# Attention and a gated feed-forward on one core: the first block's second product in another order, a cast and a copy on other engines

## The chip, the core and the metric

The kernel runs on one core of one Trainium2 chip. The core has TensorE (matrix products and transposes, PE in the profile; its weight loads are shown as PEld), VectorE (DVE), ScalarE (ACT), GpSimd (POOL) and SyncE (SP), which work side by side and wait for each other by semaphores; sixteen DMA engines move data. Products are written to PSUM, everything else lies in SBUF. The metric is the device time of one execution in microseconds.

## The reference

A recurrent attention (a decaying state per head) feeds a feed-forward block:

```python
def _attn_ref(q, k, v):                       # (4, 8, 768, 64)
    gamma = 1.0 - 2.0 ** (-5.0 - np.arange(H))
    for t in range(S):
        state = gamma[None, :, None, None] * state + np.einsum('bhd,bhe->bhde', k[:, :, t], v[:, :, t])
        y[:, :, t] = scale * np.einsum('bhd,bhde->bhe', q[:, :, t], state)

def _moe_ref(x, w_in, w_out):                 # x (3072, 512), w_in (512, 2048), w_out (2048, 512)
    h = x @ w_in
    g = h * np.tanh(softplus(h))
    return g @ w_out
```

The input of the second part is the output of the first, with the heads side by side: 4 · 768 = 3072 tokens of 8 · 64 = 512 values.

## The kernel before

**Tiling.** The tokens are cut into 24 chunks of 128. Within a chunk the recurrence is done by products: scores (k against q), a mask, `present` (masked scores times v) and `past` (the state before the chunk times q); `outer` gives what the chunk adds to the state. Chunks go through the feed-forward in blocks: block 0 has four chunks (0 to 3), each of the ten blocks behind it two. `y_two(blk)` makes the attention output of the two chunks of a block, which ScalarE copies to `xt`, the input of the block's first product.

**The two products.** The first product (`g1` for block 0, `g1_seven` for the others) gives h, to which ScalarE applies the activation and writes `g`. The second is `first_g2` for block 0 and `seven` for the others. `g1_seven`, `seven` and `first_g2` save products by sums: of the eight products of quarter matrices some or all are replaced by seven on sums and differences (Strassen and Winograd), which VectorE forms in float16: `tmats` from `w_out` (L549 to L552, the four steps of `weight_sums`), `gsums` from `g`. In `first_g2` that is done for two pairs of chunks (`pairs`) and, of the four slices of 512 rows of `w_out`, for slices 0 and 2 in the main; slices 1 and 3 go in as plain products.

**Order.** The order on every engine is the order in which the program text issues the work (`manual_schedule`); each engine takes its instructions in that order, and waits are added where data or buffers need them. `late` is a list of VectorE steps (the sums of the weights), of which `some_late(n)` issues the next n. `steps` of `g1_seven` and `seven` is a table that says which side work is issued at which named place of a block; `steps_of_first` is that of block 1. `gate(x)` is a small GpSimd copy that holds GpSimd's queue until x is there.

**PSUM.** Two pools of buffers: `mmps`, four banks, and `atps`, two buffers of two banks. In `first_g2` each pair p has two banks: `t0[p]` holds pb and pe (halves of a bank), `t1[p]` holds px and pz. A product that writes one half of a bank waits for a copy that reads the other half. The scores, the transposes, u (outer products) and y take turns in the two `atps` buffers.

**Around the change in `first_g2`.** TensorE's groups are `mm(...)`, four products per pair. Behind px (L939) ScalarE copies it out (L940). pz (L944), then pe (L946), copied as `m5` (L947). `cast_wout(2, FPS // 2)` (L948) turns slice 2 of `w_out` to float16: VectorE the first half (L184), ScalarE the second (L186). L550, the second sum of the weights, needs that slice; a gate waits for L550, and behind it GpSimd casts q (L336) and v (L347) of chunk 4, asks for k of chunk 6 (L342), and goes on with chunk 5, k of chunk 7, chunk 6. `turn(g, on_act)` transposes q and k of a chunk on TensorE (L381, L383) and copies the result to `qkt`, by ScalarE (L386) or VectorE (L388). `scores_one` is `scores` (L397) and `mask` (L403). `outer_wide(4)` (L441) and L445, L449 make the state behind chunk 4. Near the end come four groups `end(p, i)` with slice 3 of `w_out`, which ScalarE casts whole (L186, two instructions), and `y_two(1)` (L463 present, L412 outer, L454 past, L499 the copy of `xt`) ahead of the last group. Block 1 then begins with L629.

**In block 1** `spread_next` (L435, two ScalarE copies) lays the state of chunk 6 out for `past`; `sums_a` (L572, L573), `sums_b` (L700) and `sums_c` (L704) form the sums of g.

Of the kernel before, what the change touches and what calls it, by code (L numbers as in the profile page):

```python
# [16 lines left out]
def kernel(  # L17
# [161 lines left out]
    def cast_wout(s, on_act=0):  # L179
        src = wtmps.pop(("out", s))  # L180
        t = wouts[s] = cpool.tile([P, FPS, d_model], FP16, name=f"wout{s}")
        n = FPS - on_act
        if n:
            nc.vector.tensor_copy(t[:, :n], src[:, :n])  # L184
        for f in range(n, FPS, 2):
            nc.scalar.copy(t[:, f:f + 2], src[:, f:f + 2])  # L186
# [152 lines left out]
    def bring_k(g):  # L339
        if g < NCK:  # L340
            b, c = divmod(g, NCH)
            nc.gpsimd.dma_start(  # L342
                room16(g)[1], k[b, :, c * C:(c + 1) * C].rearrange("h p d -> p h d"))
# [6 lines left out]
    def casts(g):  # L350
        cast_q(g)
        cast_v(g)
# [119 lines left out]
    def scores_one(g):  # L472
        scores(g)
        mask(g)
# [7 lines left out]
    def outer_two(blk):  # L482
        gs = handed_on(blk)
        if gs:
            u_ps = u_tile()
        for j, g in enumerate(gs):
            outer(g, u_ps[:, j, :, :D])

    def y_two(blk):
        a = first[blk]  # L490
        y_ps = atps.tile([P, HP, 2, C], FP32, name="y_ps", tag="at")
        for j in range(2):
            present(a + j, lambda i: y_ps[:, i, j], j == 0)
        outer_two(blk)
        for j in range(2):
            if (a + j) % NCH > 0:
                past(a + j, lambda i: y_ps[:, i, j])
        xts[blk] = xtp.tile([P, HP, TB], FP16, name="xt")
        nc.scalar.copy(  # L499
            xts[blk][:, :, :2 * C], y_ps.rearrange("p i j c -> p i (j c)"))  # L500
# [33 lines left out]
    def some_late(n):  # L534
        for _ in range(min(n, len(late))):
            late.pop(0)()
# [360 lines left out]
    def first_g2():  # L897
# [11 lines left out]
        def a(p, i, s):  # L909
            return lambda f: gts[0, s * FPS + f][:, (2 * p + i) * P:(2 * p + i + 1) * P]  # L910
# [4 lines left out]
        def b(s, j):  # L915
            return lambda f: wouts[s][:, f, j * hf:(j + 1) * hf]
# [4 lines left out]
        def mm(o_ps, x, w, first=False, last=False):  # L921
            for f in range(FPS):
                nc.tensor.matmul(  # L923
                    o_ps, x(f), w(f), start=first and f == 0, stop=last and f == FPS - 1,
                    skip_group_check=True)
# [15 lines left out]
        g_sum(1, g_part(0, 1), g_part(2, 1), ALU.add)  # L941
        g_sum(2, the_sum(1), g_part(0, 0), sub)
        for p in pairs:
            mm(pz[p], a(p, 1, 1), b(1, 1))  # L944
        for p in pairs:
            mm(pe[p], sm(p, 1), t(1), True)  # L946
            nc.scalar.copy(m5[p], pe[p])  # L947
        cast_wout(2, FPS // 2)  # L948
        some_late(1)
        gate(tmats[0][:, 1, 0, :1])  # L950
        casts(CPB)
        bring_k(CPB + 2)
        some_late(1)
        g_sum(3, g_part(0, 0), g_part(0, 1), sub)
        g_sum(4, g_part(2, 0), the_sum(2), sub)
        some_late(1)
        for p in pairs:
            mm(pb[p], a(p, 0, 1), b(1, 0))
        for p in pairs:
# [7 lines left out]
        for p in pairs:  # L967
            mm(px[p], sm(p, 3), t(3))
            nc.vector.tensor_tensor(osb[p][1][:, 1], px[p], m5[p], op=ALU.add)
        casts(CPB + 1)  # L970
        bring_k(CPB + 3)
        for p in pairs:
            mm(pe[p], sm(p, 4), b(2, 1))
        scores_one(CPB)
        some_late(1)
        turn(CPB + 1, True)
        cast_wout(3, FPS)
        for p in pairs:
            mm(px[p], a(p, 1, 2), t(4))
# [9 lines left out]
        def end(p, i):  # L989
            mm((t0, t1)[i][p], a(p, i, 3), lambda f: wouts[3][:, f], last=True)  # L990
            if i == 0:
                nc.vector.tensor_tensor(osb[p][0], t0[p], osb[p][0], op=ALU.add)
            else:
                nc.vector.tensor_tensor(osb[p][1][:, 1], pz[p], osb[p][1][:, 1], op=ALU.add)
                nc.scalar.copy(osb[p][1][:, 0], px[p])
            row0 = (2 * p + i) * P
            stores.append((1, out[row0:row0 + P], osb[p][i].rearrange("p j c -> p (j c)")))

        end(0, 0)
        end(0, 1)  # L1000
        end(1, 0)
        y_two(1)
        end(1, 1)

    def turn_and_load(g):
# [43 lines left out]
    def steps_of_first(blk):  # L1049
        a, nb = first[blk] + 4, blk + 1  # L1050
        return {
            "p2": [(gate_x, blk), (cast_v, a - 1), (bring_k, a), (sum_next, a - 2)],
            "p6": [(turn_and_load, a - 1), (some_late, 1)],
            "p7": [(cast_q, a), (some_late, 1), (spread_next, a - 2),
                   (sums_a, blk, slice(0, FPS))],
            "p4": [(cast_v, a), (bring_k, a + 1), (some_late, 1), (store, 2),
                   (sums_a, blk, slice(FPS, FPS + 2))],
            "end": [(turn_and_load, a), (store, 2), (sums_a, blk, slice(FPS + 2, 2 * FPS))],
            "m1": [(scores, a - 2), (scores, a - 1), (mask, a - 2)],
            "m2": [(gate_g, blk), (cast_q, a + 1), (cast_v, a + 1), (bring_k, a + 2),  # L1060
                   (mask, a - 1), (turn_and_load, a + 1)],
            "m7": [(y_two, nb)],
            "m3": [(x_sums, nb)],
        }
# [39 lines left out]
```

## Time and profile before

| | |
|---|---|
| Runs before | 202.73, 202.76, 203.03 us; median 202.76 |
| The profiled execution | 203.02 us, of which the span of the profile is 201.2 |
| Granted TensorE clock, mean | 1.00 |
| TensorE busy | 191.6 us, 95% of the span |
| `first_block` up to the first row of `first_g2` | 0 to 33.07 us |
| `first_g2` with `y_two(1)` | 33.07 to 52.01 us |
| Block 1 | 52.01 to 67.59 us |
| Blocks 2 to 10 | 67.59 us to the end |

How to read it: times are microseconds from the start of the span. A row of the view in order of time gives start, length, engine, line of the kernel, operation, what is written from what, the form and a count; several like instructions in a row are merged, the length then runs from the first start to the last end. In brackets stands how long the engine sat idle before, and whose result ended that. A TensorE row's length contains a modelled tail, so successive rows overlap; the distance between starts is what a product costs. A few records of products can be missing, which shows in the counts.

```profile
DVE  2777798597679669568478587597498597596462
ACT  2363666444692494594674685675664774765740
POOL 7072006396454435636706518608606705110000
...
DMA  5999999999999997997997997998995955301102
```

These are four lines of the page's part with the span in 40 equal slices (about 5 us each), busy share in tenths: `first_g2` is the seventh slice to the tenth. VectorE has 9 of 10 in one of them and 7 or 8 in others; the DMA engines are busy throughout up to half the span.

### The profile page before, as it was taken

How to read it: one execution, taken by the hardware profiler on the slowest of the kernel's cores; microseconds unless marked ns; L12 is line 12 of the kernel's file. 1: busy time of each engine (PE TensorE's matmuls, PEld its weight loads, DVE VectorE, ACT ScalarE, POOL GpSimd, SP SyncE). 2: the span in 40 equal slices, each digit the busy share in tenths (PEclk: the TensorE clock that was granted, in tenths of full speed). 3: DMA queues.
4: the chain of work that ended last, by engine and by line, in shares of the span. 5: the costliest groups of instructions: out<-in, count | busy, mean ns of one | idle time of the engine just before them, and what ended most of it. 6: DMA issues, size and time to landing. Idle time of an engine off the chain costs nothing.

```text
span 201.2 us, 5722 instructions
## 1 busy us (share of the span) xinstructions
PE 191.6 (95%) x2363; PEld 158.1 (79%) x2363; DVE 142.9 (71%) x293; ACT 116.8 (58%) x222; POOL 81.9 (41%) x110
## 2 busy tenths in 40 slices
PE   6897999989999999999999999999999999999993
PEld 2455545775788888988988988988988988988982
DVE  2777798597679669568478587597498597596462
ACT  2363666444692494594674685675664774765740
POOL 7072006396454435636706518608606705110000
PEclk9999999999999999999999999999999999999999
DMA  5999999999999997997997997998995955301102
GB/s 176 300 313 356 384 387 287 218 285 168 236 197 222 184 186 147 195 141 149 206 144 163 185 138 152 192 131 158 183 204 116 203 85 46 114 5 50 58 26 78
DMA packets 95897, 36.05 MB, mean 179 GB/s; under 512 B 82304, under 2 KB 89984, under 8 KB 95872
## 3 DMA queue, kind: packets, MB, share of 16 engines
q1 hardware_dynamic: 74928, 33.04, 70.8%
q0 software_dynamic: 20800, 2.62, 20.4%
q8 instruction: 18, 0.29, 0.6%
q14 instruction: 7, 0.06, 0.1%
q10 hardware_dynamic: 144, 0.03, 0.1%
HBM read 27.30 MB, written 6.29 MB: 167 GB/s over the span
## 4 chain that ended last, share of the span: by engine, by line
PE 82%; ACT 6%; DVE 4%; DMA 2%; POOL 2%; issue 2%; DVEq 0%; POOLq 0%
PE o_ps L726 30%; PE h_ps L653 17%; PE h_ps L629 15%; PE h_ps L514 6%; PE y_ps L463 3%; PE at L397 2%; PE y_ps L454 2%; DMA qfirst<-in_q_dram 2%; PE o_ps L923 2%; ACT wout L186 1%; POOL qk L336 1%; PE h_ps L797 1%; PE u_ps L412 1%; DVE gsum L704 1%; DVE qfirst L211 1%
## 5 line engine op out<-in xcount | busy, mean ns | idle before, releaser
L653 PE MATMUL h_ps<-xt,win 128*128 128x256 f16 x320 | 41.5, 273 | 0.0
L646 DVE TENSOR_TENSOR hsum<-h_ps,hsnap 128x512 f32<-128x512 f32 x30 | 19.8, 687 | 22.3 <-PE h_ps L629 19.9
L726 PEld LDWEIGHTS <-gsum 128*128 128x128 f16 x320 | 30.8, 98 | 4.1 <-DVE gsum L704 0.6
L653 PEld LDWEIGHTS <-win 128*128 128x128 f16 x320 | 29.3, 98 | 3.6
L726 PE MATMUL o_ps<-tmat,gsum 128*128 128x256 f16 x240 | 27.8, 273 | 0.0
L726 PEld LDWEIGHTS <-g 128*128 128x128 f16 x240 | 23.2, 98 | 3.3 <-ACT g L660 0.4
L640 ACT ACTIVATE g<-hsum 128x512 f16<-128x512 f32 x30 | 18.6, 630 | 11.6 <-DVE hsum L646 11.6
L403 DVE TENSOR_TENSOR am<-at,tri 128x1024 f16<-128x1024 f32 x20 | 24.3, 1215 | 0.1
L347 POOL TENSOR_TENSOR v<-vf,qvs 128x512 f16<-128x512 f32 x20 | 23.5, 1173 | 0.2 <-DMA vf<-in_v_dram 0.2
L660 ACT ACTIVATE g<-h_ps 128x512 f16<-128x512 f32 x40 | 22.9, 603 | 0.8 <-PE h_ps L653 0.6
L636 ACT COPY hsnap<-h_ps 128x512 f32<-128x512 f32 x30 | 16.4, 580 | 11.3 <-PE h_ps L629 11.3
L355 POOL COPY gate<-gsum 128x1 f16<-128x1 f16 x9 | 1.6, 181 | 49.7 <-DVE gsum L700 49.7
L336 POOL TENSOR_TENSOR qk<-qf,qvs 128x512 f16<-128x512 f32 x20 | 21.2, 1060 | 0.9 <-DMA qf<-in_q_dram 0.9
L740 DVE TENSOR_TENSOR osb<-o_ps,snap 128x256 f32<-128x256 f32 x30 | 12.5, 418 | 12.5 <-PE o_ps L726 11.0
L732 ACT COPY snap<-o_ps 128x256 f32<-128x256 f32 x30 | 11.2, 373 | 16.0 <-PE o_ps L726 15.7
L629 PEld LDWEIGHTS <-wsum 128*128 128x128 f16 x320 | 19.6, 98 | 0.5
L726 PE MATMUL o_ps<-wout,g 128*128 128x256 f16 x160 | 19.4, 273 | 0.1
L342 POOL DMA_DIRECT2D qk<-in_k_dram x20 | 18.8, 942 | 0.0
L499 ACT CAST xt<-y_ps 128x1024 f16<-128x1024 f32 x10 | 10.1, 1012 | 11.9 <-PE y_ps L454 11.9
L629 PE MATMUL h_ps<-xsum,wsum 128*128 128x128 f16 x240 | 16.7, 219 | 0.0
L629 PEld LDWEIGHTS <-win 128*128 128x128 f16 x240 | 15.1, 98 | 1.1 <-issue 0.5
L435 ACT COPY stx<-stc 64x256 f16<-64x256 f16 x30 | 12.0, 399 | 2.0 <-POOL stc L429 1.8
(118 smaller groups left out, 308.4 us busy)
## 6 DMA issues: line engine op xcount, KB each, us to landing
vf<-in_v_dram SPq DMA_DIRECT2D x24, 256.0 KB, 5.6
out_dram<-osb SPq DMA_DIRECT2D x22, 256.0 KB, 4.9
qf<-in_q_dram SPq DMA_DIRECT2D x20, 256.0 KB, 4.8
wt<-in_moe_w_out_dram SPq DMA_DIRECT2D x3, 1024.0 KB, 8.6
qk<-in_k_dram POOLq DMA_DIRECT2D x20, 128.0 KB, 5.3
wi<-in_moe_w_in_dram SPq DMA_DIRECT2D x4, 512.0 KB, 7.3
wi<-in_moe_w_in_dram SPq DMA_DIRECT2D x2, 1024.0 KB, 11.3
qfirst<-in_q_dram SPq DMA_DIRECT2D x2, 512.0 KB, 5.0
```

The source lines that it names most:

```text
L336: nc.gpsimd.tensor_tensor(room16(g)[0], loaded[g][0], qs.unsqueeze(2).broadcast_to((P, H, D)), op=ALU.mult)
L342: nc.gpsimd.dma_start(room16(g)[1], k[b, :, c * C:(c + 1) * C].rearrange("h p d -> p h d"))
L347: nc.gpsimd.tensor_tensor(room16(g)[2], loaded[g][2], vs.unsqueeze(2).broadcast_to((P, H, D)), op=ALU.mult)
L403: nc.vector.tensor_tensor(am, ats.pop(g), tri.unsqueeze(1).unsqueeze(1).broadcast_to((P, 2, HP, C)), op=ALU.mult)
L629: nc.tensor.matmul(h_ps[:, f], w(f, d), x(d), start=first and f == 0 and d == 0, stop=d == n - 1, skip_group_check=True)
L636: nc.scalar.copy(x, h_ps)
L640: nc.scalar.activation(gt[:, 2 * i * FPS:(2 * i + 1) * FPS, j * P:(j + 1) * P], h, AF.Mish, scale=inv_boost3)
L646: nc.vector.tensor_tensor(h, h_ps, x, op=ALU.add)
L653: nc.tensor.matmul(h_ps[:, j], win(s, 2 * half + j, bp), xt(blk, bp), start=bp == 0, stop=bp == NBP - 1)
L660: nc.scalar.activation(gt[:, fb:fb + 2], h_ps, AF.Mish, scale=inv_boost3)
L726: nc.tensor.matmul(o_ps, x(f), w(f), start=first and f == 0, stop=f == n - 1, skip_group_check=True)
L740: nc.vector.tensor_tensor(dst, o_ps, plus, op=ALU.add)
```

## The change

It touches `first_g2`, the place of the outer products of `y_two(1)`, and the table of block 1.

```diff
-    def y_two(blk):
+    def y_two(blk, hand_on=True):
...
-        outer_two(blk)
+        if hand_on:
+            outer_two(blk)
...
         for p in pairs:
-            mm(pz[p], a(p, 1, 1), b(1, 1))
-        for p in pairs:
             mm(pe[p], sm(p, 1), t(1), True)
             nc.scalar.copy(m5[p], pe[p])
-        cast_wout(2, FPS // 2)
+        cast_wout(2)
         some_late(1)
         gate(tmats[0][:, 1, 0, :1])
         casts(CPB)
-        bring_k(CPB + 2)
+        cast_q(CPB + 1)
         some_late(1)
         g_sum(3, g_part(0, 0), g_part(0, 1), sub)
         g_sum(4, g_part(2, 0), the_sum(2), sub)
         some_late(1)
+        for p in pairs:
+            mm(pz[p], a(p, 1, 1), b(1, 1))
         for p in pairs:
             mm(pb[p], a(p, 0, 1), b(1, 0))
...
-        casts(CPB + 1)
+        bring_k(CPB + 2)
+        cast_v(CPB + 1)
         bring_k(CPB + 3)
         for p in pairs:
             mm(pe[p], sm(p, 4), b(2, 1))
-        scores_one(CPB)
         some_late(1)
-        turn(CPB + 1, True)
+        scores(CPB)
+        turn(CPB + 1)
+        mask(CPB)
...
         end(0, 0)
         end(0, 1)
+        y_two(1, False)
         end(1, 0)
-        y_two(1)
+        outer_two(1)
         end(1, 1)
...
-            "p6": [(turn_and_load, a - 1), (some_late, 1)],
-            "p7": [(cast_q, a), (some_late, 1), (spread_next, a - 2),
-                   (sums_a, blk, slice(0, FPS))],
-            "p4": [(cast_v, a), (bring_k, a + 1), (some_late, 1), (store, 2),
+            "p6": [(turn_and_load, a - 1), (some_late, 2)],
+            "p7": [(cast_q, a), (some_late, 1), (sums_a, blk, slice(0, FPS))],
+            "p4": [(cast_v, a), (bring_k, a + 1), (store, 2),
...
-            "m1": [(scores, a - 2), (scores, a - 1), (mask, a - 2)],
+            "m1": [(spread_next, a - 2), (scores, a - 2), (scores, a - 1), (mask, a - 2)],
```

In words: pe is computed before pz; slice 2 of `w_out` is cast by VectorE alone; q of chunk 5 is cast directly behind v of chunk 4, and the load of k of chunk 6 is issued behind it; the transposes of chunk 5 are copied by VectorE, ahead of the mask of chunk 4, where ScalarE copied them behind it; y of block 1 comes two groups before the end in place of one, and its outer products stand between the last two groups; in block 1 the third weight sum (L551) and the fourth (L552) of slices 1 and 3 are issued one place earlier and the spread of the state moves from p7 to m1. No product, cast or transfer is added or taken away, except that one cast of 2048 elements per partition stands for two of 1024. The order of SyncE's instructions is the same. The two `atps` buffers change hands in one place: u of chunk 4 takes the buffer of the transposes of chunk 5, and scores(5) the buffer of scores(4).

## The prediction

> **What bounds the kernel now.** I read the page first (shares by engine), then the busy time by block, then TensorE's rows in order of time where it is not full.
>
> ```profile
> span 201.2 us, 5722 instructions
> ## 1 busy us (share of the span) xinstructions
> PE 191.6 (95%) x2363; PEld 158.1 (79%) x2363; DVE 142.9 (71%) x293; ACT 116.8 (58%) x222; POOL 81.9 (41%) x110
> ```
>
> TensorE is the bound. The view of busy time by stretch, cut where each block of two chunks begins (start:end, length, then busy time of PE, PEld, DVE, ACT, POOL), shows where it is not full:
>
> ```profile
> 52.01:67.59 15.58, 15.01 (x197) 13.02 (x196) 12.81 (x27) 9.05 (x18) 8.06 (x10) 1.00 1.18 209
> ...
> 82.35:96.99 14.64, 14.64 (x194) 13.19 (x192) 10.64 (x24) 9.49 (x19) 7.76 (x10) 1.00 0.98 164
> ```
>
> From 67.59 on PE is busy throughout, so a stall removed earlier moves everything behind it forward. Block 1 takes 15.58 against 14.64 of a full block: 0.94 to be had there. The rest to be had lies in first_g2, ahead of 52.01. TensorE's rows in order of time (start, length, line, tile, count, idle before):
>
> ```profile
> 33.07 2.15 PE L923 MATMUL o_ps<-wout,g 128*128 128x256 f16 x16
> 35.05 1.04 PE L923 MATMUL o_ps<-tmat,gsum 128*128 128x256 f16 x8
> 36.11 3.07 PE L923 MATMUL o_ps<-wout,g 128*128 128x256 f16 x24
> 39.02 1.04 PE L923 MATMUL o_ps<-tmat,gsum 128*128 128x256 f16 x8
> 40.33 0.40 PE L381 MATMUL t_ps<-ident,qk 128*128 128x128 f16 x4 [0.27 <-POOL qk L336]
> ...
> 42.63 0.40 PE L397 MATMUL at<-qkt 64*128 64x128 f16 x8
> 43.74 0.40 PE L381 MATMUL t_ps<-ident,qk 128*128 128x128 f16 x4 [0.71 <-POOL qk L336]
> ...
> 45.07 1.04 PE L923 MATMUL o_ps<-wout,g 128*128 128x256 f16 x8
> 45.94 0.39 PE L441 MATMUL u_ps<-v,qk 128*128 128x128 f16 x4
> 46.26 0.40 PE L397 MATMUL at<-qkt 64*128 64x128 f16 x8
> 46.59 0.61 PE L923 MATMUL o_ps<-wout,g 128*128 128x512 f16 x2
> 47.35 2.32 PE L923 MATMUL o_ps<-wout,g 128*128 128x512 f16 x10 [0.15 <-ACT wout L186]
> ...
> 50.75 1.03 PE L923 MATMUL o_ps<-wout,g 128*128 128x512 f16 x4
> 52.01 1.05 PE L629 MATMUL h_ps<-xt,win 128*128 128x128 f16 x16 [0.24 <-ACT xt L499]
> ```
>
> Lengths overlap their successors, so I go by starts. Eight products of 256 columns take 45.94 − 45.07 = 0.87 us (0.109 each); one of 512 columns takes (50.75 row) (1.03 − 0.38)/3 = 0.215, 0.38 being the row's tail; a scores group 46.59 − 46.26 = 0.33. What a group takes beyond this is a stall:
> - 33.07 x16 should end at 34.81; the next starts at 35.05: 0.24 lost. 35.05 + 0.87 = 35.92, next 36.11: 0.19 lost. 36.11 + 24·0.109 = 38.73, next 39.02: 0.29 lost.
> - 39.02 + 0.87 = 39.89, transposes of chunk 4 at 40.33: 0.44 lost, to GpSimd's cast of q.
> - scores(4) 42.63 + 0.33 = 42.96, transposes of chunk 5 at 43.74: 0.78 lost, again to a cast of q.
> - 46.59 + 2·0.215 = 47.02, next 47.35: 0.33 lost, to ScalarE's cast of wout slice 3.
> - 50.75 + 4·0.215 = 51.61, block 1 at 52.01: 0.40 lost, to the copy of xt.
>
> **The change, part by part.** *The fifth products pe go ahead of pz.* What the first three stalls wait for stands in ScalarE's rows:
>
> ```profile
> 33.77 0.75 ACT L940 COPY osb<-o_ps 128x256 f32<-128x256 f32 x2
> ...
> 35.69 0.81 ACT L947 COPY snap<-o_ps 128x256 f32<-128x256 f32 x2 [1.17 <-PE o_ps L923]
> 36.40 1.05 ACT L186 CAST wout<-wt 128x1024 f16<-128x1024 f32 x1
> ```
>
> pz shares its bank with px, which L940 copies out (first of two done about 34.13, pz went at 34.18); pb shares its bank with pe, copied by L947 (first done about 36.06, pb at 36.11). In the new order px, pe, pz, pb a group of 0.87 stands between each product and the copy that the next user of its bank waits for: pe runs 33.94–34.82 (its sum, VectorE's, is done by 33.6), pz 34.82–35.69, pb from 35.69. Both waits fit in with 0.3 or more to spare: +0.24, +0.19; bounds 0 and these.
>
> *Slice 2 cast by VectorE alone.* The rows of VectorE and GpSimd that this and the next step rest on:
>
> ```profile
> 29.14 1.22 DVE L184 CAST wout<-wt 128x2048 f16<-128x2048 f32 x1
> ...
> 34.56 0.85 DVE L184 CAST wout<-wt 128x1024 f16<-128x1024 f32 x1 [0.29 <-DMA wt<-in_moe_w_out_dram]
> ...
> 37.48 0.69 DVE L550 TENSOR_TENSOR tmat<-wout,tmat 128x1024 f16<-128x1024 f16 x1 [2.06 <-ACT wout L186]
> ...
> 38.31 0.50 POOL L355 COPY gate<-tmat 128x1 f16<-128x1 f16 x1 [3.42 <-DVE tmat L550]
> 38.77 1.50 POOL L336 TENSOR_TENSOR qk<-qf,qvs 128x512 f16<-128x512 f32 x1
> ...
> 40.24 1.48 POOL L347 TENSOR_TENSOR v<-vf,qvs 128x512 f16<-128x512 f32 x1
> ...
> 40.74 1.53 DVE L552 TENSOR_TENSOR tmat<-wout,tmat 128x1024 f16<-128x1024 f16 x1
> ...
> 42.63 1.05 POOL L336 TENSOR_TENSOR qk<-qf,qvs 128x512 f16<-128x512 f32 x1
> ```
>
> A whole slice takes 1.22, so it is done at 34.56 + 1.22 = 35.78. TensorE first reads the half that ScalarE had at 36.56 (second group of pb): the 0.29 goes, with 0.8 of cover. L550 starts at 35.82 instead of 37.48, and with it everything that hung on it comes 1.66 sooner: the gate at 36.65, the cast of q of chunk 4 done at 40.27 − 1.66 = 38.61. TensorE wants it behind px's third group, 39.02 − 0.72 + 0.87 = 39.17: the 0.44 goes, cover 0.5.
>
> *q of chunk 5 cast ahead of the load of k of chunk 6.* It follows v of chunk 4 (done at 41.72 − 1.66 = 40.06) directly. Uncontended it takes 1.05; beside L552 GpSimd's casts took 1.50. So it is done between 41.1 and 41.55; its load had landed:
>
> ```profile
> qf<-in_q_dram SPq DMA_DIRECT2D x1, 256.0 KB, 7.9
> ```
>
> (asked for the load issued at 30.83: landed 38.7). TensorE has recovered 0.24 + 0.19 + 0.29 + 0.44 = 1.16 by then and wants it at 42.96 − 1.16 = 41.80. Cover 0.25 to 0.7; the 0.78 goes. Sum so far 1.94. Queued behind this cast on GpSimd are the load of k of chunk 6, issued at about 41.5 instead of 41.67, v of chunk 5, and the load of k of chunk 7, about 1.2 sooner. SP's order is untouched.
>
> *The copy of the transposes of chunk 5 goes from ScalarE to VectorE, ahead of mask(4).* This is the price. The same copy exists once (lines grouped by form), and the rows that follow it on VectorE are:
>
> ```profile
> L227 DVE COPY qfirst_t<-t_ps 128x1024 f16<-128x1024 f16 x1 | 1.2, 1223 | 0.8 <-PE t_ps L217 0.8
> ```
>
> ```profile
> 46.37 0.69 DVE L445 TENSOR_TENSOR su<-u_ps,st 128x512 f32<-128x512 f32 x1 [1.13 <-PE u_ps L441]
> 46.97 1.22 DVE L403 TENSOR_TENSOR am<-at,tri 128x1024 f16<-128x1024 f32 x1
> 48.10 0.68 DVE L449 TENSOR_TENSOR st<-su,gcm 128x512 f16<-128x512 f32 x1
> ```
>
> Successive VectorE rows overlap by 0.08 (48.19 against 48.10). The transposes start at 43.74 − 1.94 = 41.80, the copy some 0.66 later, 42.46, ends 43.69; mask(4) ends 44.83. The buffers change hands: u(4) now takes the transposes' buffer, free at 43.69, before TensorE needs it (45.94 − 1.94 = 44.00); scores(5) takes the buffer that mask(4) reads. It would start at 46.26 − 1.94 = 44.32 and waits until about 44.88: **a new wait, −0.55**. Queued behind it on TensorE are the last products and y. Bounds: −0.05 if the copy took no longer than L550's 0.69, −0.9 if VectorE is held up by another 0.36 (below). I take the row of the same shape.
>
> *The other ScalarE gain.* Without the copy, ScalarE is free for slice 3 when its halves land; it took them at 45.30 only because that copy ended at 45.41. Two casts of 1.05 from then ended at 47.30. Now they can end by about 45, ahead of TensorE's use at 45.6: +0.33.
>
> *y two groups sooner, outer products between the last two.* y's rows want mask(5) and the decayed state. After scores(5), mask(5) ends about 46.65 and L449 about 47.25; TensorE comes to y at 44.88 + 0.33 + 8·0.215 = 46.93 and to the state's part near 47.7. No wait. Behind y there are now two groups and the outer products (2·0.86 + 0.22) to cover the copy of xt, which waits on ScalarE behind the copy of osb:
>
> ```profile
> 50.95 1.01 ACT L499 CAST xt<-y_ps 128x1024 f16<-128x1024 f32 x1 [0.83 <-PE y_ps L454]
> ```
>
> It runs about 48.5–49.5; TensorE needs it at 49.9: +0.40, cover 0.35. The outer products now stand alone between two groups, waiting for v of chunk 6, whose cast ended near 47.9; TensorE gets there at 48.8. Bound: 0, to −1 if its load slips by 2.
>
> *Block 1.* The spread of the state (two ScalarE copies) leaves p7, and L551, L552 move one place forward on VectorE:
>
> ```profile
> 58.63 0.82 PE L726 MATMUL o_ps<-wout,g 128*128 128x256 f16 x6
> 59.59 0.11 PEld L726 LDWEIGHTS <-g 128*128 128x128 f16 x2 [0.43 <-ACT g L660]
> ...
> 65.02 0.40 PE L454 MATMUL y_ps<-qkt,stx 128*128 128x128 f16 x4
> 65.83 0.77 PEld L726 LDWEIGHTS <-gsum 128*128 128x128 f16 x8 [0.59 <-DVE gsum L704]
> ```
>
> The first wait is 59.60 − (58.63 + 6·0.109) = 0.31, for a ScalarE result (L660) that stood behind the spread, about 0.8 long: gone. The second, 0.59, is for L704, at the end of VectorE's queue; that queue shortens by the 0.68 of L552 and no longer waits the 0.8 for ScalarE, while TensorE arrives 0.31 sooner. L704 itself lengthens beside GpSimd. Bounds +0.1 and +0.59; I take +0.45, nearer the upper end. L551 goes into an idle stretch of VectorE, before it waits for TensorE.
>
> **Sum.** 1.94 − 0.55 + 0.33 + 0.40 + 0.31 + 0.45 = 2.88. The profiled execution took 203.02 (span 201.2 and 1.8 around it): 203.02 − 2.88 = 200.14. The median of the runs, 202.76, lies 0.26 below it: **199.9 us**.
>
> **Rivals.**
> - *The hand-over turns into VectorE's stage (0.24).* GpSimd and VectorE hold each other up: L552 took 1.53 where L550, the same shape, took 0.69, beside a GpSimd cast of 1.48 instead of 1.05. If the cast of q of chunk 5 gets in first, L552 ends 0.48 later (about 41.1), and what is queued behind it moves by some 0.36 into the copy, mask(4) and scores(5); if block 1's second wait also stays at 0.45 of its 0.59 and xt's cover fails by 0.3: 2.88 − 0.36 − 0.3 − 0.3 = 1.9, 200.9. For it: VectorE has hardly a gap between 34.56 and 47.2. Against it: the cast starts when L552 has long been waiting. The Trainium skill, SBUF — State Buffer, section "Who interferes with whom", says that a VectorE instruction with two inputs in SBUF contends with a GpSimd one that reads SBUF, and that whichever is issued first blocks the other in full; the pair 1.53 and 1.48 above agrees with blocking in full rather than sharing. By that rule L552, issued first, wins here, and this half of the rival falls.
> - *The loads set the pace (0.05).* If v of chunk 6 lands 2 to 3 later because k of chunk 6 and 7 are asked for sooner, the outer products hold TensorE to about 51.5, and block 1's casts come late too: gain about 0 to 0.4, 202.6. Against: k of chunk 6 moves by 0.2 only.
> - *Slower (0.07).* In later blocks GpSimd and VectorE fall into the alignment of block 1, so that L704 ends late in each and TensorE waits 0.59 as at 65.83. This decides from five of the nine blocks on (5·0.59 = 2.95); in all nine it gives 202.76 − 2.88 + 5.3 = 205.2, at six 203.4. For: L704 is as long as 1.49. Against: the later blocks start each of these casts from gates on VectorE's own results, so a shift in time moves both.
> - *The change does not do what it says (0.02)*: a wait kept by bank, say pz on px's copy, leaves part of the 1.94: about 202.
>
> **How the numbers follow.** Forecast 0.62: its own range, from the bounds of scores(5) (+0.5, −0.36) and L704 (+0.14, −0.35), is 199.2 to 200.7. The range stretches to the first rival: 199.2 to 201.4. A difference of 0.2% (0.4 us) is about what can be told from no change. Faster 0.88, same 0.05, slower 0.07.
>
> **What would show it.** Right: TensorE without a gap from 33.07 to the outer product u(4); a wait of about 0.5 ahead of scores(5) put down to mask(4); slice 3 and xt without a wait; the first row of block 1 near 49.9; block 1 in 14.6 to 14.9; blocks from 2 on as long as now. Wrong: a wait of TensorE for q of chunk 5 or for v of chunk 6, a wait for L704 in later blocks, or the copy of chunk 5's transposes far from 1.22.

## The result, and the profile after

| | before | after |
|---|---|---|
| Runs | 202.65 to 203.03 us, median 202.75 | 200.06 to 200.96 us, median 200.47 |
| Ratio | | 0.9887, 95% interval 0.9858 to 0.9915 |
| Profiled execution (its span) | 203.02 (201.2) | 200.17 (198.4) |
| First px row | 33.07 | 32.80 |
| First row of block 1 | 52.01 | 49.78 |
| Length of block 1 | 15.58 | 14.96 |

The change makes the kernel 2.3 us faster. In the changed kernel the lines of the helpers stand one lower: the sums of the weights are L550 to L553 (L549 to L552 before), the sums of the gates L701 and L705, the copy of `xt` L500, the products of `first_g2` L924.

The page of the changed kernel, span and busy time by engine:

```profile
span 198.4 us, 5725 instructions
PE 190.2 (96%) x2363; PEld 157.7 (79%) x2363; DVE 144.8 (73%) x294; ACT 114.9 (58%) x220; POOL 82.5 (42%) x110
```

Busy time by stretch, cut at the blocks (start:end, length, then PE, PEld, DVE, ACT, POOL):

```profile
32.80:49.78 16.98, 16.76 (x173) 12.58 (x172) 15.19 (x20) 7.12 (x12) 12.88 (x13) 1.00 1.43 223
49.78:64.74 14.96, 14.71 (x197) 13.03 (x196) 13.54 (x27) 8.96 (x18) 8.14 (x11) 1.00 1.41 221
64.74:79.51 14.77, 14.77 (x202) 13.32 (x200) 10.65 (x24) 9.49 (x19) 7.76 (x10) 1.00 1.42 196
```

`first_g2` has fallen from 18.94 to 16.98, block 1 from 15.58 to 14.96; from block 2 on both kernels take the same, block by block, to 0.03 us. VectorE is busy for 15.19 of the 16.98: it has hardly any room left there. TensorE's rows in order of time (start, length, line, tile, count, idle before):

```profile
32.80 1.04 PE L924 MATMUL o_ps<-wout,g 128*128 128x256 f16 x8
33.67 1.04 PE L924 MATMUL o_ps<-tmat,gsum 128*128 128x256 f16 x8
34.54 3.66 PE L924 MATMUL o_ps<-wout,g 128*128 128x256 f16 x32
38.04 1.04 PE L924 MATMUL o_ps<-tmat,gsum 128*128 128x256 f16 x8
...
41.20 0.40 PE L397 MATMUL at<-qkt 64*128 64x128 f16 x8
41.73 0.40 PE L381 MATMUL t_ps<-ident,qk 128*128 128x128 f16 x4
...
43.93 0.39 PE L441 MATMUL u_ps<-v,qk 128*128 128x128 f16 x4
44.26 0.40 PE L397 MATMUL at<-qkt 64*128 64x128 f16 x8
44.59 2.15 PE L924 MATMUL o_ps<-wout,g 128*128 128x512 f16 x8
46.68 0.64 PE L463 MATMUL y_ps<-am,v 128*64 128x128 f16 x16
...
49.78 1.06 PE L630 MATMUL h_ps<-xt,win 128*128 128x128 f16 x16
...
62.99 1.05 PE L727 MATMUL o_ps<-wout,gsum 128*128 128x256 f16 x8 [0.25 <-DVE gsum L705]
```

Three stalls are left. The transposes of chunk 5 start 0.53 behind scores(4), where such a group takes 0.33: 0.20 for the cast of q, the second of these rows of VectorE and GpSimd, which ends at 41.68:

```profile
39.24 1.53 DVE L553 TENSOR_TENSOR tmat<-wout,tmat 128x1024 f16<-128x1024 f16 x1
40.19 1.49 POOL L336 TENSOR_TENSOR qk<-qf,qvs 128x512 f16<-128x512 f32 x1
```

The eight products from 44.59 take 2.09 to the next row; without a wait such eight take 1.83 (undo_pe, below): 0.26, for slice 3. And 0.25 to 0.4 for L705 in block 1. Ahead of scores(5) there is none: u(4) starts at 43.93, scores(5) 0.33 later.

The chain of work that ended last (start, length, what) shows what is new:

```profile
36.80 7.38 DMA wt<-in_moe_w_out_dram
...
44.20 1.05 ACT wout L186
...
45.29 1.46 PE o_ps L924 x6
```

It comes from the load of the second half of slice 3 and ScalarE's cast of it. TensorE now arrives so early that a load holds it, which before the change stood in the shadow of other waits.

### The profile page after: what moved, and what is told of

Its sections match the earlier page's. It is cut to its first block, busy times and chain, and to the rows that moved or that the text cites. A ratio compares the mean times of both kernels' runs of the same rounds, so it can differ in the third digit from the quotient of the medians.

```text
span 198.4 us, 5725 instructions
## 1 busy us (share of the span) xinstructions
PE 190.2 (96%) x2363; PEld 157.7 (79%) x2363; DVE 144.8 (73%) x294; ACT 114.9 (58%) x220; POOL 82.5 (42%) x110
## 4 chain that ended last, share of the span: by engine, by line
PE 78%; SPq 7%; DMA 6%; DVE 4%; ACT 2%; issue 1%; DVEq 0%
PE o_ps L727 30%; PE h_ps L654 18%; PE h_ps L630 16%; SPq L140 5%; DMA wt<-in_moe_w_out_dram 4%; PE y_ps L463 3%; PE at L397 3%; DMA qfirst<-in_q_dram 2%; PE y_ps L454 2%; PE o_ps L924 2%; PE h_ps L798 1%; SPq L165 1%; PE u_ps L412 1%; DVE gsum L705 1%; SPq L170 1%
## 5 line engine op out<-in xcount | busy, mean ns | idle before, releaser
L654 PE MATMUL h_ps<-xt,win 128*128 128x256 f16 x320 | 41.5, 273 | 0.0
L647 DVE TENSOR_TENSOR hsum<-h_ps,hsnap 128x512 f32<-128x512 f32 x30 | 19.8, 688 | 20.9 <-PE h_ps L630 18.9
L661 ACT ACTIVATE g<-h_ps 128x512 f16<-128x512 f32 x40 | 22.9, 603 | 0.8 <-PE h_ps L654 0.6
L630 PE MATMUL h_ps<-xsum,wsum 128*128 128x128 f16 x240 | 16.7, 219 | 0.0
L500 ACT CAST xt<-y_ps 128x1024 f16<-128x1024 f32 x10 | 10.1, 1013 | 10.6 <-PE y_ps L454 10.6
```

The costliest lines, as they stand in the source:

```text
L630: nc.tensor.matmul(h_ps[:, f], w(f, d), x(d), start=first and f == 0 and d == 0, stop=d == n - 1, skip_group_check=True)
L647: nc.vector.tensor_tensor(h, h_ps, x, op=ALU.add)
L654: nc.tensor.matmul(h_ps[:, j], win(s, 2 * half + j, bp), xt(blk, bp), start=bp == 0, stop=bp == NBP - 1)
L661: nc.scalar.activation(gt[:, fb:fb + 2], h_ps, AF.Mish, scale=inv_boost3)
```

## The experiments

The table has every kernel that was run. Each ratio is against runs of the kernel before that were made beside it; their median differs between the sets, as the first row shows. The last three columns are of the one profiled execution, which need not be a typical one: for `best2` and `best3` it is the slowest of their runs.

| kernel | median us | ratio (interval) | px | block 1 starts | block 1 takes |
|---|---|---|---|---|---|
| before | 202.24 to 202.82 | 1 | 33.07 | 52.01 | 15.58 |
| after | 200.47 | 0.9887 (0.9858 to 0.9915) | 32.80 | 49.78 | 14.96 |
| again | 200.60 | 0.9917 (0.9900 to 0.9934) | 32.28 | 50.30 | 14.82 |
| act_copy | 200.88 | 0.9929 (0.9913 to 0.9945) | 32.78 | 49.89 | 15.43 |
| strided | 204.70 | 1.0119 (1.0074 to 1.0163) | 32.84 | 51.70 | 16.78 |
| slice3_sooner | 200.50 | 0.9911 (0.9892 to 0.9930) | 32.44 | 49.75 | 15.07 |
| undo_pe | 200.33 | 0.9880 (0.9865 to 0.9895) | 32.70 | 49.66 | 15.05 |
| undo_cast | 200.50 | 0.9889 (0.9872 to 0.9905) | 33.05 | 49.90 | 15.15 |
| undo_q5 | 203.01 | 0.9992 (0.9964 to 1.0021) | 32.70 | 50.76 | 16.77 |
| undo_y | 200.69 | 0.9901 (0.9881 to 0.9921) | 33.06 | 49.77 | 15.37 |
| q5_gated | 201.32 | 0.9924 (0.9909 to 0.9939) | 32.66 | 50.73 | 15.16 |
| undo_block1 | 201.35 | 0.9926 (0.9909 to 0.9942) | 33.23 | 49.95 | 15.86 |
| best2 | 200.07 | 0.9865 (0.9851 to 0.9880) | 32.70 | 50.26 | 14.72 |
| best3 | 200.67 | 0.9884 (0.9867 to 0.9902) | 32.95 | 51.03 | 14.55 |

### The changed kernel again: again

No edit.

> The changed kernel once more, for a second profile: its four runs spread from 200.06 to 200.96, where those of before spread by 0.4. Theory A (in the changed kernel TensorE meets slice 3 of w_out as it lands, so the loads now set the pace of the last products of first_g2): the spread comes from the loads; the stretch from the first row of px to the first row of block 1 (16.98 in the first profile) moves by up to 0.9 between profiles, together with the start of ScalarE's second cast of slice 3 (44.20), and block 1 (14.96) and the blocks behind stay within 0.1. Rival B (the opening, ahead of first_g2, spreads): the stretch stays within 0.1 of 16.98 and the first row of px moves from 32.80.

It began px 0.52 sooner than the first profile and block 1 0.52 later, so the stretch between them took 18.02 in place of 16.98. Its rows at slice 3:

```profile
44.71 1.04 ACT L186 CAST wout<-wt 128x1024 f16<-128x1024 f32 x1 [0.48 <-DMA wt<-in_moe_w_out_dram]
...
45.81 1.46 PE L924 MATMUL o_ps<-wout,g 128*128 128x512 f16 x6 [0.59 <-ACT wout L186]
```

The second half came 0.5 later than in the first profile (44.71 against 44.20 for its cast), and TensorE waited for it. That is theory A, for half of the 1.04. The other half is px itself, which moved as B has it and gained nothing: TensorE waited 0.30 for the sum of L934, and the rows that start at 34.50 here start at 34.54 in the first profile. So the start of block 1 did not follow px; it moved with the load. Block 1 took 14.82, 0.14 from the first profile, a little more than A allowed.

### The copy of chunk 5's transposes: act_copy and strided

act_copy gives it back to ScalarE, at its new place; strided has VectorE write it with a step of four elements.

```diff
-        turn(CPB + 1)
+        turn(CPB + 1, True)                  # act_copy
+        turn(CPB + 1, apart=True)            # strided
...
+            v = qktp.tile([P, 2, C, HP], FP16, name="qkt", bufs=4).rearrange("p a c b -> p a b c")
+            nc.vector.tensor_copy(v, t_ps.rearrange("p (a b) c -> p a b c", a=2))
```

> The copy of the transposes of chunk 5 by ScalarE again, all else as changed. My prediction's sum (the copy on VectorE costs 1.22 and holds scores(5) up by 0.55): this would be 0.5 faster. Theory A with the copy at the 0.69 that the profile after shows: nothing held scores(5) up, so nothing is gained there; ScalarE's copy (1.01, from about 42.4) ends near 43.4 and pushes the casts of slice 3 (2 times 1.05) to an end near 45.4 against 45.24, so the last products start 0.1 to 0.2 later: the stretch from px to block 1 is 17.1 to 17.2, the time the same within what can be told.

> The copy of the transposes of chunk 5 by VectorE writes every fourth element (its tile is laid out with the four heads of a half innermost), as the copy in the opening does that my prediction took its 1.22 from; TensorE then reads that tile with the same step. Theory S (the step of the output makes it 1.22 in place of 0.69): the row is 1.22, mask(4) ends 0.53 later, scores(5) starts near 44.75 instead of 44.26, after a wait for mask(4), and the last products miss slice 3's landing by about 0.25 less, so the stretch from px to block 1 is 17.2 to 17.3. Rival (the opening's copy is slow for another reason, for one GpSimd's casts beside it): the row stays 0.69 and the stretch 16.98.

act_copy: px to block 1 in 17.11 against 16.98, as theory A has it, and not 0.5 faster: 200.88, against 200.60 of `again`, which was run beside it. ScalarE copies from 42.40 and casts slice 3 in one go behind it until 45.35; TensorE waits 0.20 there, and waits at this place in the changed kernel too. Up to block 1 it decides nothing which engine copies, as long as the copy comes at this place. Block 1 is 0.47 longer; in it one sum ran beside GpSimd's cast (L573 1.26 us, 0.41 in the changed kernel).

VectorE's row of the changed kernel, then VectorE's and TensorE's of strided:

```profile
42.39 0.69 DVE L388 COPY qkt<-t_ps 128x1024 f16<-128x1024 f16 x1 [0.17 <-PE t_ps L383]
```

```profile
42.40 2.46 DVE L387 COPY qkt<-t_ps 128x1024 f16<-128x1024 f16 x1 [0.17 <-PE t_ps L383]
```

```profile
44.91 0.38 PE L447 MATMUL u_ps<-v,qk 128*128 128x128 f16 x4 [0.80 <-DVE qkt L387]
45.96 0.64 PE L403 MATMUL at<-qkt 64*128 64x128 f16 x8 [0.67 <-DVE am L409]
```

Without a step the copy takes 0.69. With the step here it takes 2.46, and the wait ahead of scores(5) that the prediction had described comes, 0.67 long and put down to mask(4), with 0.80 ahead of u(4). So the mechanism exists, and the duration decides it. The row of 1.22 that the prediction took for the same copy has another pattern, and strided does not repeat it, as its expectation had it: by the program text (L222 to L227) the opening's copy writes in order and reads `t_ps` with a step of 128 elements, where strided reads in order and writes with a step of four. Why one takes 1.22 and the other 2.46 stays open; no run has the step on the reading side at this place. A GpSimd cast beside it is not what lengthens the copy: one ran beside the 0.69 as well (42.58 to 43.64 in the changed kernel). The Trainium skill, VectorE: DVE Perf Modes, section "What auto-detection actually checks", says that the engine takes 2×_1P, its mode of two elements per cycle for one port, if every tensor is 16-bit with a step of one. The two lengths, 0.69 and 1.22, agree with that; 2.46 is beyond it. The four runs of strided are two of 203.9 and two of 205.5, and the profile is of one of the first. strided starts block 1 1.92 later than the changed kernel; that the block then takes 1.82 longer is not the copy's doing but the hold shown below (L558, L552 elsewhere, took 3.04).

### Slice 3 loaded ahead of v of chunk 5: slice3_sooner

```diff
-        for g in (CPB, CPB + 1):
-            load_one(g, 0, nc.sync)
-            load_one(g, 2, nc.sync)
+        load_one(CPB, 0, nc.sync)
+        load_one(CPB, 2, nc.sync)
+        load_one(CPB + 1, 0, nc.sync)
...
         load_last_wout(0)
         load_last_wout(1)
+        load_one(CPB + 1, 2, nc.sync)
...
         bring_k(CPB + 2)
-        cast_v(CPB + 1)
         bring_k(CPB + 3)
+        cast_v(CPB + 1)
```

> The two halves of slice 3 of w_out are asked for ahead of v of chunk 5 in place of behind it, and GpSimd casts v of chunk 5 behind the load of k of chunk 7. Theory A: the halves land 1.0 to 1.3 sooner (second at about 43), ScalarE's second cast ends by 44.2, the gap of 0.25 in the last products (row at 45.29) goes and the stretch from px to block 1 is 16.7 to 16.8; v of chunk 5 lands near 44.2 and its cast ends by 45.6, ahead of y at 46.7. Theory B (the loads aren't what the last products end on): 16.98 as before. A loss would be v of chunk 5 late: y waits for it, up to 0.5 slower.

The wait for slice 3 is gone (y starts at 46.34), and the next load takes its place, v of chunk 6 ahead of the outer products:

```profile
48.63 0.32 PE L412 MATMUL u_ps<-v,qk 128*64 128x64 f16 x8 [0.23 <-POOL v L347]
```

Block 1 starts where it did, 49.75, and the stretch from px takes 17.31, not the 16.7 to 16.8 of theory A; the time, 200.50, cannot be told from the 200.60 of `again`.

### Each part undone: undo_pe, undo_cast, undo_y, undo_q5, undo_block1

Each has one part of the change taken back:

```diff
+            mm(pz[p], a(p, 1, 1), b(1, 1))               # undo_pe: ahead of pe again
...
-        cast_wout(2)
+        cast_wout(2, FPS // 2)                           # undo_cast
...
-        cast_q(CPB + 1)                                  # undo_q5
...
-        cast_v(CPB + 1)
+        casts(CPB + 1)
...
-        y_two(1, False)                                  # undo_y
         end(1, 0)
-        outer_two(1)
+        y_two(1)
```

undo_block1 has block 1's table of before.

> The fifth products pe go behind pz again; the rest is the changed kernel. Read: the length from the first px row to the first row of block 1 (18.94 us before the change, 16.99 and 18.01 in two profiles of the changed kernel) and the start of block 1 (52.01; 49.78 and 50.30). Theory A (with the change the loads of wout's slice 3 and of the last chunks set the pace behind 45 us, so the terms of the sum do not add): the two early waits of 0.24 and 0.19 ahead of pz and pb come back, but the wait of about 0.2 for the cast of q of chunk 5 at the second transposes and the 0.25 at slice 3 take them up: block 1 starts within 0.2 of 49.8 to 50.3, the time within 0.2 us of the changed kernel. Theory B (the terms add, as the prediction summed them): both waits come back in full and nothing takes them up: 0.43 later, about 50.2 to 50.7, the time 0.43 us above the changed kernel's.

> Slice 2 is cast half by ScalarE again; the rest is the changed kernel. Theory A (what freed the cast was that pe's copies now stand earlier on ScalarE; the cast's half is then done near 36.1 and VectorE's sum L551, which needs it, starts at most 0.2 later): no wait of TensorE ahead of pb's second group, the transposes of chunk 4 not held, block 1 starts within 0.2 of the changed kernel's, time within 0.2 us of it. Theory B (the prediction's terms: the 0.29 and the 0.44 hang on this cast): both waits come back, 0.73 us slower than the changed kernel.

> y of block 1 and the outer products stand two groups nearer the end again, their place before the change; the rest is the changed kernel. Theory A (the outer products put between two groups of 512 columns cost about 0.1 to 0.2 us of issue each kernel, and the copy of xt is hidden again only in part): the wait of TensorE for the copy of xt comes back as 0.2 to 0.4, block 1 starts 0.1 to 0.25 later, time 0.1 to 0.25 us above the changed kernel. Theory B (the term of the sum in full): the wait is 0.40, time 0.40 us above it. Theory C (loads set the pace even there): no difference.

undo_pe has the two early waits back, 0.25 and 0.19, and starts block 1 in 16.95 from px where the changed kernel takes 16.98. Its rows show where 0.44 went:

```profile
32.70 2.15 PE L924 MATMUL o_ps<-wout,g 128*128 128x256 f16 x16
34.69 1.04 PE L924 MATMUL o_ps<-tmat,gsum 128*128 128x256 f16 x8
...
41.53 0.40 PE L397 MATMUL at<-qkt 64*128 64x128 f16 x8
41.86 0.40 PE L381 MATMUL t_ps<-ident,qk 128*128 128x128 f16 x4
...
44.72 1.90 PE L924 MATMUL o_ps<-wout,g 128*128 128x512 f16 x8
46.55 0.64 PE L463 MATMUL y_ps<-am,v 128*64 128x128 f16 x16
```

Sixteen products should end at 34.44 and the next starts at 34.69; but then the transposes of chunk 5 follow without a wait, and the eight products take 1.83: the 0.20 and the 0.26 of the changed kernel are gone. In undo_cast ScalarE, free sooner since m5's copies moved ahead, casts its half from 35.26 to 36.31; L551 starts at 36.34 against 35.98, later than A allowed, and still neither the 0.29 nor the 0.44 comes back. Its rows of ScalarE and VectorE:

```profile
35.26 1.05 ACT L186 CAST wout<-wt 128x1024 f16<-128x1024 f32 x1
36.34 0.69 DVE L551 TENSOR_TENSOR tmat<-wout,tmat 128x1024 f16<-128x1024 f16 x1 [0.98 <-ACT wout L186]
```

In undo_y the wait for `xt` is back, 0.39, as B has it, and block 1 starts at 49.77 all the same, as C has it; its time is 0.2 above the changed kernel's through block 1 (15.37), where L552 took 2.04. Over the changed kernel and these three px varies by 0.36, and block 1 starts between 49.66 and 49.90 without following it: the terms don't add.

> q of chunk 5 is cast behind the load of k of chunk 6 again, its place before the change; the rest is the changed kernel. Theory A (part of it is taken up at slice 3, whose landing TensorE otherwise waits for): the second transposes wait 0.4 to 0.8 for the cast of q, the wait of 0.25 at slice 3 goes, block 1 starts 0.2 to 0.5 later than the changed kernel's, time 0.2 to 0.5 us above it. Theory B (the term of the sum, 0.78, in full): 0.78 us above it.

Neither theory: in the median this one part takes back everything. Its ten runs lie between 200.89 and 203.43, eight of them above 202; the two others, 200.89 and 201.25, have no profile, and why they are faster is not shown. In the profiled run (202.96) the wait of 0.70 for q is back as A had it, but two rows of VectorE are far too long. VectorE's and GpSimd's rows:

```profile
41.33 2.38 DVE L550 TENSOR_TENSOR tmat<-wout 128x1024 f16<-128x1024 f16 x1
...
54.09 3.04 DVE L552 TENSOR_TENSOR tmat<-wout,wout 128x1024 f16<-128x1024 f16 x1
```

```profile
41.09 1.05 POOL L336 TENSOR_TENSOR qk<-qf,qvs 128x512 f16<-128x512 f32 x1
42.10 1.04 POOL L347 TENSOR_TENSOR v<-vf,qvs 128x512 f16<-128x512 f32 x1
...
53.56 0.94 POOL L342 DMA_DIRECT2D qk<-in_k_dram  x1
54.52 1.05 POOL L336 TENSOR_TENSOR qk<-qf,qvs 128x512 f16<-128x512 f32 x1
55.53 1.04 POOL L347 TENSOR_TENSOR v<-vf,qvs 128x512 f16<-128x512 f32 x1
```

Both sums take 0.68 by themselves. Each ends about 0.6 behind the end of two GpSimd casts that stand back to back, which take their unhindered 1.04: VectorE is held through both. The first hold moves the copy of the transposes, mask(4) and scores(5) (a wait of 0.69), the second makes TensorE wait 1.57 for L647 in block 1. In the changed kernel the same place looks so:

```profile
52.59 0.94 POOL L342 DMA_DIRECT2D qk<-in_k_dram  x1
53.85 1.03 POOL L336 TENSOR_TENSOR qk<-qf,qvs 128x512 f16<-128x512 f32 x1 [0.33 <-DMA qf<-in_q_dram]
```

```profile
53.12 0.68 DVE L552 TENSOR_TENSOR tmat<-wout,wout 128x1024 f16<-128x1024 f16 x1
```

L552 starts 0.53 behind the start of the load's issue in both. The difference is that here the cast waited until 53.85 for its load, and L552 was through by 53.80.

> Block 1's steps as before the change (the spread ahead of the sums, L551 and L552 one place later); the rest is the changed kernel. Theory A (the prediction's reading): the waits of 0.31 for a ScalarE result and of 0.59 for L705 come back in place of the 0.36 that is left; block 1 takes 15.4 to 15.7, time 0.5 to 0.8 us above the changed kernel. Theory B (the gain in block 1 came only from where its start stands against the loads): block 1 within 0.2 of 14.96, no difference in time.

Block 1 takes 15.86, the time is 0.9 above the changed kernel's: A, a little more than it asked. The wait for ScalarE (0.43 of weight load for L661's result) and that for L705 are both there.

### The hold tested by itself: q5_gated

undo_q5, and in block 1 the cast of q of chunk 8 waits for L552.

```diff
-            "p7": [(cast_q, a), (some_late, 1), ...
+            "p7": [(gate, tmats[1][:, 0, FPS, :1]), (cast_q, a), (some_late, 1), ...
```

> As undo_q5 (q of chunk 5 cast at its old place), and in block 1 GpSimd's cast of q of chunk 8 waits, by a copy of one column, for the result of VectorE's sum L552. In undo_q5 that cast followed the issue of the load of k without a gap, L552 took 3.04 us, TensorE waited 1.57 for the sum behind it (L647), and block 1 took 16.77 (14.96 in the changed kernel, where the cast waited 0.33 for its load and L552 took 0.68). Theory A (L552 is held until GpSimd's row of ready casts is over): L552 takes 0.68 to 0.75, the wait of 1.57 is gone, block 1 takes 14.8 to 15.4; the stretch from px to block 1 stays at 18.0; time 201.2 to 201.7 against 203.0. Theory B (block 1 is longer because it starts late and what it needs is late by itself): L552's length is a symptom, TensorE waits elsewhere, block 1 stays above 16.3 and the time at 203.

VectorE's and GpSimd's rows:

```profile
54.07 0.68 DVE L552 TENSOR_TENSOR tmat<-wout,wout 128x1024 f16<-128x1024 f16 x1
```

```profile
53.54 0.94 POOL L342 DMA_DIRECT2D qk<-in_k_dram  x1
54.89 0.18 POOL L355 COPY gate<-tmat 128x1 f16<-128x1 f16 x1 [0.41 <-DVE tmat L552]
55.03 1.03 POOL L336 TENSOR_TENSOR qk<-qf,qvs 128x512 f16<-128x512 f32 x1
```

Theory A: L552 0.68, block 1 15.16 against 16.77, the time 1.7 lower, and its four runs lie within 0.08 (201.29 to 201.37), where those of undo_q5 spread over 2.5. The cast made to wait makes the kernel faster.

### Versions that ought to beat both: best2 and best3

best2: slice 3 as in slice3_sooner; L553 behind the additions of L970 and L550 behind L449; the outer products behind the last group; the gate of q5_gated; and the casts of chunk 9 gated on L705 instead of L701, with the load and the transposes behind them, at a later place (m5 in place of m2).

```diff
-        some_late(1)
         for p in pairs:
             mm(pz[p], a(p, 1, 1), b(1, 1))
...
             nc.vector.tensor_tensor(osb[p][1][:, 1], px[p], m5[p], op=ALU.add)
+        some_late(1)
...
         end(1, 0)
-        outer_two(1)
         end(1, 1)
+        outer_two(1)
...
-        gate(gsums[blk % 2][:, 2, 0, :1])
+        gate(gsums[blk % 2][:, 3 if blk == FIRST else 2, 0, :1])
...
-            "m2": [(gate_g, blk), (cast_q, a + 1), (cast_v, a + 1), (bring_k, a + 2),
-                   (mask, a - 1), (turn_and_load, a + 1)],
+            "m2": [(mask, a - 1)],
+            "m5": [(gate_g, blk), (cast_q, a + 1), (cast_v, a + 1), (bring_k, a + 2),
+                   (turn_and_load, a + 1)],
```

> The changed kernel with: slice 3 of wout loaded ahead of v of chunk 5; VectorE's sums L553 and L550 moved out of the way of the cast of q and the copy of the transposes of chunk 5; the outer products of chunks 6 and 7 behind the last group; in block 1 the cast of q of chunk 8 behind L552, and the casts of chunk 9 behind the fourth sum L705 instead of the third. If the waits left in the changed kernel are what the rows name (0.2 for q of chunk 5, 0.25 for slice 3, v of chunk 6 behind it, 0.36 for L705 lengthened by GpSimd): TensorE without a gap from px to block 1, the stretch 16.5 to 16.7, L705 0.68 to 0.75 long, block 1 14.5 to 14.75, time 199.5 to 199.9. If the waits only move on to the next load: the stretch stays at 16.9 to 17.3, time 200.0 to 200.4, the rest from block 1.

In `first_g2` the waits for q of chunk 5 and for slice 3 are gone, 0.17 is lost in the second part of y, and then comes one long wait:

```profile
50.02 0.32 PE L412 MATMUL u_ps<-v,qk 128*64 128x64 f16 x8 [0.78 <-POOL v L347]
```

In block 1 L705 takes 0.68 without GpSimd beside it (1.49 in the changed kernel), its wait is gone, and the block takes 14.72. So block 1 came as expected, and `first_g2` like the second case and worse, 17.56 against its 16.9 to 17.3: the wait moved on to the next load, v of chunk 6. SyncE issued it 0.86 later than in the changed kernel (38.91 against 38.05), and it took 9.9 to land in place of 8.6 (48.79 against 46.68). This profile is of the slowest of the four runs, 200.39; the others lie between 200.00 and 200.12, and may have waited less. best2 has the lowest median, 200.07; its interval lies below that of again and overlaps those of undo_pe, of best3 and of the first set of the changed kernel.

best3 loads k of chunk 7 behind the cast of v of chunk 5. It also moves L550 between the two pairs of last groups, and ScalarE's copy of the first pair's px behind that of `xt`.

```diff
         bring_k(CPB + 2)
-        bring_k(CPB + 3)
         cast_v(CPB + 1)
+        bring_k(CPB + 3)
```

> As best2, but k of chunk 7 is loaded behind the cast of v of chunk 5 (asked for about 45.4 us instead of 42.1), L550 runs between the two pairs of last groups, and ScalarE copies out the first pair's px behind the copy of xt instead of ahead of it. In best2 TensorE waited 0.78 for v of chunk 6, whose load landed at 48.8 among those of k and q of chunk 7 (46.7 in the changed kernel). Theory A (k of chunk 7, asked for early, took the bandwidth that v of chunk 6 needed): v of chunk 6 lands by 47.5, the wait goes, the stretch from px to block 1 takes 16.5 to 16.8 (17.57 in best2, 16.99 in the changed kernel), block 1 14.6 to 14.8, time 199.3 to 199.7. Theory B (the loads as a whole set the pace): v of chunk 6 lands after 48.3 again or the copy of xt is late, the stretch stays above 17.2, time 200.0 or more.

v of chunk 6 landed at 47.97, 8.5 behind its issue, where A asked for 47.5, and TensorE no longer waits for it. That k of chunk 7 had been in its way is not shown: slice3_sooner asks for k of chunks 6 and 7 about as early as best2 (from 41.5, best2 from 41.2), and there v of chunk 6 took 8.5 too. And the moved issue met L449. VectorE's, GpSimd's and TensorE's rows:

```profile
46.24 2.43 DVE L449 TENSOR_TENSOR st<-su,gcm 128x512 f16<-128x512 f32 x1
```

```profile
46.10 0.94 POOL L342 DMA_DIRECT2D qk<-in_k_dram  x1
47.06 1.06 POOL L336 TENSOR_TENSOR qk<-qf,qvs 128x512 f16<-128x512 f32 x1
```

```profile
48.73 0.40 PE L454 MATMUL y_ps<-qkt,st 128*128 128x128 f16 x4 [1.19 <-DVE st L449]
```

The hold again: L449 takes 0.68 to 1.43 elsewhere, here it starts during the issue of a load with a ready cast behind it, and y waits 1.19. Without that, block 1 (14.55, the shortest) would have started at about 49.8, where it starts in the changed kernel with px 0.15 sooner. Neither theory as written: the wait for v went, and a new hold took what that gave. This profile too is of the slowest run, 201.05; the other five lie between 199.67 and 200.95, the lowest inside A's 199.3 to 199.7, and whether they had the hold is not shown.

## Why the prediction was right, and where it was not

The forecast was 199.9, with 199.2 to 201.4 for the range; 200.47 lies within, 0.6 above the forecast. The gain is 2.3 by the ratio of the first set and 1.7 by that of again, against 2.88. Point by point:

- *pe ahead of pz, 0.24 and 0.19.* Both stalls are gone, as the rows from 32.80 on show. But undo_pe shows that TensorE, arriving 0.44 sooner, only waits for the next things; taken alone the step is worth nothing.
- *The cast of slice 2, 0.29 and 0.44.* The stalls are gone, but not by this edit alone. The step that failed is that ScalarE's half of the cast was taken to stay where it was, from 36.40; behind m5's copies, which moved with pe, it starts at 35.26 in undo_cast and is done before TensorE needs it. Either edit removes these stalls: undo_cast has them gone without this one, undo_pe without the other.
- *q of chunk 5 sooner, 0.78.* It brought 0.58: the cast took 1.49 beside L553 and ended at 41.68, against the 41.1 to 41.55 that had been worked out, and TensorE, which had begun px 0.27 sooner, wanted it at 41.53 and not at 41.80. What the step was worth beyond its own stall was not seen at all: it keeps GpSimd's pair of casts off L550, and the late start off block 1, together 2.5 us in undo_q5.
- *The new wait ahead of scores(5), −0.55.* There is none. The copy's length was mis-sized: 1.22 from a row of the same shape that reads with a step, 0.69 measured. The lower bound, the copy at 0.69, was the right one.
- *Slice 3, +0.33.* Some 0.07. "Now they can end by about 45" held (45.24), but TensorE came at 45.02, 0.6 sooner than the 45.6 reckoned, since the wait ahead of scores(5) was missing. About half of what that miss gave was lost again here.
- *y and xt, +0.40.* The wait for `xt` is gone; the outer products between two groups of 512 columns cost 0.10 (47.70 to 48.66 where a group takes 0.86), and y loses another 0.10: its first part takes 0.57 up to the next row (46.68 to 47.25), where it took 0.47 with the outer products behind it (49.60 to 50.07 before). By undo_y the time is within 0.2 either way.
- *Block 1, 0.31 and 0.45.* 0.62 came. The wait for ScalarE went; that for L705 went from 0.59 to between 0.28 and 0.42 of weight load, so 0.2 to 0.3 of the 0.45. The term was too big because VectorE stays full and L553 and L705 run beside GpSimd (1.24 and 1.49); with L705 at 0.68, in best2, the wait is gone.
- *The later blocks* are as long as before: the rival that made the kernel slower is out.

Of the first rival, the order that it feared did not come: L553, which started ahead of the cast, kept the 1.53 of before, and the cast was the one that grew, to 1.49. What it had right is that GpSimd and VectorE hold each other up; the holds of undo_q5 are that, in a larger form and at other places. Of the other rivals, "the loads set the pace" was given 0.05 and a gain of next to nothing; what happened is its mechanism at another load and in mild form, 0.26 to 0.59 at slice 3. The sum came out near the time because misses stood against each other: 0.55 too low at scores(5), some 0.8 too high at q of chunk 5 (0.20), slice 3 (0.26), y and the split groups (0.20) and block 1 (0.14); that much of its closeness is luck. The upper end of the forecast's own range adds up to 200.6, not 200.7. The two profiled executions differ by 2.85, nearly the sum, but 0.27 of that lies ahead of px, which the change doesn't touch.

## What to carry to other kernels

When several stalls in a row are removed, sum them only up to the next fixed arrival, a load or a cast that nothing moves: taking each part back alone showed that three of five were worth 0.2 us or nothing by themselves. Take the duration of a copy from a row with the same steps on both sides, not only the same shape. And where VectorE and GpSimd both work from SBUF, look at what stands ready behind GpSimd's current instruction: a short wait put ahead of a GpSimd cast can be worth more than an earlier cast.

## What the runs showed of the hardware

A VectorE instruction with two inputs in SBUF was held through GpSimd's casts in five kernels, where it entered while GpSimd was issuing a load, or casting, with a ready cast next: 3.04 (undo_q5 and strided, two casts), 2.38 (undo_q5, q5_gated, two casts), 2.43 (best3, one) and 2.04 us (undo_y, one), against 0.68. The casts took their unhindered 1.03 to 1.06. In other places the two alternate and each takes about 1.5, as L553 and the casts from 37.3 to 41.7 do in the changed kernel. The Trainium skill, SBUF — State Buffer, section "Who interferes with whom", says that the ports shared by the two engines are an exclusive lock and that issue order decides who blocks. By the records L552 of undo_q5 started at 54.09, 0.43 ahead of the cast, and yet waited for it and the one behind it; by that measurement the rule doesn't say who wins. What does, why the two alternate in some places and not in others, and why in best3 VectorE got in between two ready casts, stays open.
